# Logits of a soft mixture of experts: the token values as TensorE weights, the folded output columns moving

## The chip, the core and the metric

The kernel runs on one core of a Trainium2 chip. The core has a matrix engine (TensorE, PE in the rows; its weight loads are listed apart as PEld), a vector engine (VectorE, DVE), a scalar engine (ScalarE, ACT), a general one (GpSimd, POOL) and a queue that issues DMAs (SyncE, SP). A matmul on TensorE holds one operand still as weights and streams the other through it column by column; its result goes to PSUM, from which DVE and ACT read. The metric is the device time of one execution in microseconds, as the median of several.

## What is computed

Three stages: attention with query pooling, a gated unit (SiLU), and a soft mixture of experts whose dispatch and combine weights are two softmaxes of the same logits.

```python
def _moe_ref(x, w_gate, w_val, w_out):            # x: 2304 tokens x 512
    g = x @ w_gate                                # 512 x 1536
    silu = g * (1.0 / (1.0 + np.exp(-g)))
    return silu * (x @ w_val) @ w_out             # 1536 x 512

def _moe2_ref(x, phi, w1, w2):                    # phi: 512 x 32
    logits = x @ phi                              # 2304 x 32
    d = softmax(logits, over tokens)              # dispatch
    slot_input = d.T @ x                          # 32 slots x 512
    slot_out = relu(slot_input @ w1) @ w2         # 8 experts, 4 slots each
    c = softmax(logits, over slots)               # combine
    return c @ slot_out
```

## The kernel before

The 16 attention steps (4 batches, 4 pairs of heads) run first, each some 40 us long. From step 4 on the gated unit is woven into them, by a pace table that says how many of its pieces are due by which step; what is left runs alone after the last step. The experts come at the end ("the tail").

The gated unit goes through the 2304 tokens in 9 blocks of 256 tokens, and in a block through 6 slices of 256 hidden units (`block_slice`). A slice is 24 matmuls for g and 24 for v (lines 738, 742, 743: 128x256 values moving through 128x128 weights), then a tanh on ACT (749), three element-wise steps on DVE (750, 761, 779) and a cast on ACT (777). They leave the slice's values `h` as a high half `hh` in bfloat16 and a low half `hs[:, 1]` in float16, 128 hidden units on the partitions, two such groups `ci`, 256 tokens along the free axis. A slice's values go two ways:

- By a transposing DMA (780) into `Hn`, which holds a whole block. At the block's end `block_sums` multiplies it by the dispatch weights (matmuls `G`, line 905, added up into `G_acc` on DVE, 910). There is one buffer of `Hn` and there are two of `hs`.
- Into the logits, through `W2S`: w_out times phi, folded beforehand, as a high and a low half of 32 columns each, so 64 columns for a group of 128 hidden units. `slice_logits` (and `slice_last` for the last slice of all) issues four matmuls into a PSUM tile `lp` and DVE adds that to `La` (820, 822; 804 for the last).

In the logits matmuls of before the columns of `W2S` are the weights and the 256 tokens move: group 0 lands on PSUM partitions 0 to 63, group 1 on 64 to 127, and the 32 columns for the low halves on 0 to 31 and 64 to 95. So `La` is 128 partitions of 256 tokens, with four partial sums of each logit on four groups of 32 partitions. `SELW`, a stack of four scaled identities, adds the four up: at a block's end (`block_end`) a matmul with `SELW` as weights (846) gives `L`, 32 slots of 256 tokens, for the dispatch softmax; in `combine` a matmul for each 128 tokens with `La` as weights and `SELW` moving (920) gives `lt`, 128 tokens of 32 slots, for the combine softmax. Both are float32, which the trace shows as two instructions for each matmul.

The order of instructions on each engine isn't the order of the code: a scheduler places them by its own estimate of when each is ready, under the dependences that the code adds (`behind`, `not_before`). `stages` is a list of pieces of work that a slice leaves behind; one is issued at each step of the next slices, so that a slice's logits come while the next slice's g and v run.

Of the kernel before, what the change touches and what calls it, by code (L numbers as in the profile page):

```python
# [11 lines left out]
F32 = mybir.dt.float32  # L12
# [4 lines left out]
AF = mybir.ActivationFunctionType  # L17
ALU = mybir.AluOpType
AX = mybir.AxisListType
# [5 lines left out]
WSC = 256.0  # L25
HSC = 2.0**14
W2SC = 64.0
DSC = 1024.0
HB = 2
HI_DVE, LO_PART = 0.0, 1.0  # L30
# [33 lines left out]
MXB, STB, PVB, TRB, MMB = 2, 2, 1, 1, 2  # L64
# [13 lines left out]
def tile_pool_attention_glu_softmoe(  # L78
# [35 lines left out]
    def ps(tag, shape, dtype=F32, bufs=1, name=None):  # L114
        return psum.tile(shape, dtype, tag=tag, bufs=bufs, name=name or tag)
# [4 lines left out]
    id16 = const.tile([P, P], F16, name="id16")  # L120
    SEL = const.tile([P, NS], F32, name="SEL")
    CN = const.tile([P, 2, NS], F32, name="CN")
    SELW = const.tile([P, NS], F32, name="SELW")

    marks = []

# [9 lines left out]
    def selections():  # L136
        for z in range(P // NS):
            r = slice(z * NS, (z + 1) * NS)
            nc.gpsimd.tensor_copy(out=SEL[r, :], in_=id32[r, r])
        nc.gpsimd.tensor_scalar(SELW, SEL, 1.0 / (HSC * W2SC), None, ALU.mult)  # L140
        nc.gpsimd.memset(CN, 0.0)
        for z in range(2):
            r = slice(z * P // 2, (z + 1) * P // 2)
            nc.gpsimd.tensor_copy(out=CN[r, z, :], in_=SEL[r, :])
        nc.gpsimd.tensor_copy(out=id16, in_=id32)
# [3 lines left out]
    c_all = const.tile([P, NT // P, NS], F32, name="c_all")  # L149
    m_run = [const.tile([NS, 1], F32, name=f"m_run{i}") for i in range(2)]  # L150
    s_run = const.tile([NS, 1], F32, name="s_run")
    La = const.tile([P, BLK], F32, name="La")

    w_stack = ExitStack()
    wpool = ctx.enter_context(tc.tile_pool(name="wgv", bufs=1, side="left", reuse_waits="tile"))
# [611 lines left out]
    def behind(ins):  # L767

        if moe["done"] < late:
            after(ins, moe["mm"])  # L770

    def slice_halves(j, fp, Hn, h, hs, hh):
# [8 lines left out]
            out=Hn[:, fp].rearrange("p a c i f -> p (a c i) f"), in_=hs.rearrange("p a c n -> p (a c n)")  # L781
        ).ins.name

    def slice_last(j, fp, Hn, h, hs, hh):
        t = ps("tr", [P, BLK], bufs=TRB, name=f"lp{j}_{fp}")
        for ci in range(2):
            w = W2S[:, 2 * fp + ci]
            r = slice(ci * 2 * NS, (ci + 1) * 2 * NS)
            nc.scalar.copy(hh[:, ci, :], h[:, ci])
            if ci:  # L790
                warm(0, moe["mm_last"])
            nc.tensor.matmul(
                t[r, :], w.rearrange("p a s -> p (a s)"), hh[:, ci, :], start=True, stop=False, skip_group_check=True
            )
            nc.vector.tensor_tensor(out=hs[:, 1, ci], in0=h[:, ci], in1=hh[:, ci, :], op=ALU.subtract)
            mm = nc.tensor.matmul(
                t[ci * 2 * NS:ci * 2 * NS + NS, :], w[:, 0, :], hs[:, 1, ci, :], start=False, stop=True,
                skip_group_check=True,
            )
            moe["mm_last"] = mm  # L800
        moe["turn"] = nc.sync.dma_start_transpose(
            out=Hn[:, fp].rearrange("p a c i f -> p (a c i) f"), in_=hs.rearrange("p a c n -> p (a c n)")
        ).ins.name
        nc.vector.tensor_tensor(out=La, in0=La, in1=t, op=ALU.add)

    def slice_logits(j, fp, hs, hh):

        t = ps("tr", [P, BLK], bufs=TRB, name=f"lp{j}_{fp}")
        for ci in range(2):
            w = W2S[:, 2 * fp + ci].rearrange("p a s -> p (a s)")  # L810
            behind(nc.tensor.matmul(
                t[ci * 2 * NS:(ci + 1) * 2 * NS, :], w, hh[:, ci, :], start=True, stop=False, skip_group_check=True
            ))
        for ci in range(2):
            r = slice(ci * 2 * NS, ci * 2 * NS + NS)
            nc.tensor.matmul(
                t[r, :], W2S[:, 2 * fp + ci, 0, :], hs[:, 1, ci, :], start=False, stop=True, skip_group_check=True
            )
        if fp == 0:
            nc.vector.tensor_copy(out=La, in_=t)  # L820
        else:
            nc.vector.tensor_tensor(out=La, in0=La, in1=t, op=ALU.add)
# [16 lines left out]
    def block_end(j):  # L839
        mp = moe["pool"]  # L840
        Hn = moe[j]["Hn"]
        if j == NBLK - 1:
            warm(1, moe["mm_last"])
        tg, bf = ("mx", MXB) if j >= late else ("tr", TRB)
        L = ps(tg, [NS, BLK], bufs=bf, name=f"L{j}")
        mm = nc.tensor.matmul(L, SELW, La, start=True, stop=True)
        behind(mm)
        if j == NBLK - 1:
            warm(2, mm)

# [8 lines left out]
        nc.vector.tensor_scalar(ng, new, -1.0, None, ALU.mult)  # L859
        dT = h_tile(f"dT{j}")[1][:NS, :BLK]  # L860
        sb = mp.tile([NS, 1], F32, tag="sb", bufs=1, name=f"sb{j}")
        al = None
        if j:
            al = mp.tile([P, 1], F32, tag="al", bufs=2, name=f"al{j}")
            nc.scalar.activation(al[:NS, :], old, AF.Exp, bias=ng)
        nc.scalar.activation(dT, L, AF.Exp, bias=ng, accum_out=sb)
# [48 lines left out]

    def combine(j, mp):

        t = ps("tr", [P, 2, NS], bufs=TRB, name=f"lt{j}")
        for i in range(2):
            nc.tensor.matmul(t[:, i, :], La[:, i * P:(i + 1) * P], SELW, start=True, stop=True)  # L920
        cm = mp.tile([P, 2, 1], F32, tag="cm", bufs=1, name=f"cm{j}")
        nc.vector.tensor_reduce(out=cm, in_=t, axis=AX.X, op=ALU.max)
        ce = mp.tile([P, 2, NS], F32, tag="ce", bufs=1, name=f"ce{j}")
        nc.vector.tensor_tensor(out=ce, in0=t, in1=cm.to_broadcast([P, 2, NS]), op=ALU.subtract)
        nc.scalar.activation(ce, ce, AF.Exp)
# [380 lines left out]
```

## Time and profile before

| | before |
|---|---|
| median of 3 runs (lowest to highest) | 865.88 us (865.73 to 868.37) |
| span of the profiled execution | 863.9 us |
| PE busy, share of the span | 816.8 us, 95% |
| DVE, ACT, POOL busy | 541.2, 392.5, 414.0 us |

Times in the rows are microseconds from the span's start, in one profiled execution. Matmuls overlap: the busy time of one (0.27 us for 256 columns) is its latency, and what it takes of the engine is read from its start to the start of the next. A bracket at a row's end is the engine's idle time before it and what ended that.

### The profile page before, as it was taken

Reading aid. Unit: us, or ns where it says so; the run is one execution under the profiler, and the core shown is the slowest. Engines: PE = TensorE matmul, PEld = TensorE weight load, DVE = VectorE, ACT = ScalarE, POOL = GpSimd, SP = SyncE. Lnnn points to the kernel's source line nnn. Section 1 sums busy time; section 2 is a strip of 40 time slices with the busy share of each in tenths; the row PEclk is TensorE's granted clock in tenths of the full one; section 3 lists DMA queues with packets and bytes.
Section 4 is the critical chain, followed back from the end, with each engine's and each line's share of the span. In section 5 each row is a group of like instructions: output and inputs, shape, how many; then the busy total and the mean of one; then the engine's idle time right before and its main releaser. Section 6 shows DMA issues by size and latency. Waiting matters only on the chain.

```text
span 863.9 us, 23702 instructions
## 1 busy us (share of the span) xinstructions
PE 816.8 (95%) x9952; PEld 580.0 (67%) x9952; DVE 541.2 (63%) x1060; ACT 392.5 (45%) x739; POOL 414.0 (48%) x380
## 2 busy tenths in 40 slices
PE   5888898999999999999999999999999999998997
PEld 1455566777666767677776777676777777776345
DVE  6878779678888675666657575666723444445223
ACT  3455678677778444343434344344434211212112
POOL 7878667465768545564564556565445100000100
PEclk9999999999999999999999999999999999999998
DMA  6562678959759433424544445324012598457999
GB/s 194 149 153 84 200 214 239 284 127 280 192 173 293 115 61 82 111 76 100 130 115 120 111 107 125 65 26 97 16 28 38 149 292 267 85 165 193 297 290 292
DMA packets 151868, 132.48 MB, mean 153 GB/s; under 512 B 83152, under 2 KB 120720, under 8 KB 151760
## 3 DMA queue, kind: packets, MB, share of 16 engines
q1 hardware_dynamic: 149600, 130.92, 57.8%
q8 instruction: 78, 1.28, 0.6%
q10 hardware_dynamic: 2160, 0.04, 0.1%
q14 instruction: 30, 0.25, 0.1%
HBM read 84.10 MB, written 7.86 MB: 106 GB/s over the span
## 4 chain that ended last, share of the span: by engine, by line
PE 75%; DVE 12%; DMA 7%; ACT 3%; issue 2%; SPq 0%; ACTq 0%; DVEq 0%
PE st L462 7%; PE st L461 7%; PE mx L380 6%; PE g L738 5%; PE g L743 5%; PE g L742 5%; PE v L738 5%; PE v L743 5%; PE v L742 5%; DVE mp L386 3%; PE pv L497 3%; PE pv L505 3%; PE pv L506 3%; PE pv L507 3%; PE hp L1179 2%
## 5 line engine op out<-in xcount | busy, mean ns | idle before, releaser
L474 POOL TENSOR_TENSOR PL<-P 128x512 f16<-128x512 f32 (+1 forms) x311 | 326.0, 1061 | 230.0 <-ACT P L467 227.7
L467 ACT ACTIVATE P<-st 128x512 f32<-128x512 f32 (+1 forms) x336 | 191.4, 582 | 207.0 <-PE st L462 174.1
L386 DVE TENSOR_REDUCE mp<-mx 128x1 f32<-128x512 f32 x270 | 179.9, 684 | 55.9 <-PE mx L380 53.0
L461 PE MATMUL st<-QQ,KK 128*128 128x512 f16 (+1 forms) x576 | 143.7, 291 | 5.1 <-ACT P L467 4.3
L462 PE MATMUL st<-QH,KL 65*128 65x512 f16 (+1 forms) x576 | 144.4, 293 | 2.7 <-DMA QH<-mt 2.7
L505 PE MATMUL pv<-VV,P 128*128 128x65 f16 x1088 | 136.8, 193 | 4.9 <-DVE x L537 4.8
L506 PE MATMUL pv<-VV,P 128*128 128x64 f16 x1088 | 136.7, 195 | 0.0
L507 PE MATMUL pv<-VV,PL 128*128 128x65 f16 x1088 | 134.6, 192 | 0.0
L738 PE MATMUL g<-xT,wgv 128*128 128x256 f16 x432 | 118.6, 275 | 3.3 <-DVE hs L750 3.0
L505 PEld LDWEIGHTS <-P 128*128 128x128 bf16 x1088 | 103.9, 98 | 25.3 <-DVE x L537 6.5
L743 PE MATMUL g<-xT,wgv 128*128 128x256 f16 x432 | 118.5, 274 | 0.5 <-DVE wgv L703 0.5
L742 PE MATMUL g<-xT,wgv 128*128 128x256 f16 x432 | 118.6, 274 | 0.0
L738 PE MATMUL v<-xT,wgv 128*128 128x256 f16 x432 | 117.9, 273 | 0.0
L743 PE MATMUL v<-xT,wgv 128*128 128x256 f16 x432 | 117.8, 273 | 0.0
L742 PE MATMUL v<-xT,wgv 128*128 128x256 f16 x432 | 117.7, 273 | 0.0
L507 PEld LDWEIGHTS <-PL 128*128 128x128 f16 x1088 | 103.7, 99 | 13.5 <-issue 4.4
L506 PEld LDWEIGHTS <-P 128*128 128x128 bf16 x1088 | 103.2, 98 | 10.4 <-issue 2.2
L380 PE MATMUL mx<-kh,QD 128*128 128x512 f16 x270 | 103.8, 402 | 6.6 <-DVE mp L386 3.1
L738 PEld LDWEIGHTS <-wgv 128*128 128x128 f16 x864 | 85.1, 98 | 18.6 <-issue 2.1
L742 PEld LDWEIGHTS <-wgv 128*128 128x128 f16 x864 | 84.8, 98 | 18.4 <-issue 4.1
L743 PEld LDWEIGHTS <-wgv 128*128 128x128 f16 x864 | 84.8, 98 | 16.1 <-issue 0.8
L462 PEld LDWEIGHTS <-KL 65*128 65x128 f16 x576 | 51.7, 99 | 33.0 <-issue 14.9
(184 smaller groups left out, 1192.4 us busy)
## 6 DMA issues: line engine op xcount, KB each, us to landing
w<-in_w SPq DMA_DIRECT2D x16, 1024.0 KB, 7.6
w<-in_w SPq DMA_DIRECT2D x64, 256.0 KB, 5.5
vr<-in_vP SPq DMA_DIRECT2D x16, 585.0 KB, 5.1
KK<-kh SPq DMA_DIRECT2D x62, 144.0 KB, 2.6
qr<-in_qT SPq DMA_DIRECT2D x15, 576.0 KB, 3.9
kr<-in_kT SPq DMA_DIRECT2D x15, 576.0 KB, 4.2
r<-in_w_out SPq DMA_DIRECT2D x12, 512.0 KB, 4.3
r<-in_w_gate SPq DMA_DIRECT2D x24, 256.0 KB, 5.1
```

The source lines that it names most:

```text
L380: nc.tensor.matmul(t, q, kh[:, k0:k0 + kw], start=True, stop=True)
L386: nc.vector.reduce_max(out=mp[:, g, c:c + 1], in_=t, axis=AX.X)
L461: nc.tensor.matmul(t[:, o:o + w], KK[:, k], QQ[:, q0:q0 + w], start=True, stop=False)
L462: nc.tensor.matmul(t[:, o:o + w], KL[:, k], QH[:, q0:q0 + w], start=False, stop=True)
L467: marks.append(nc.scalar.activation(P32[:, :o], t[:, :o], AF.Exp, scale=1.0 / 16.0).ins.name)
L474: eng.tensor_tensor(out=PL[:, :o], in0=P32[:, :o], in1=PH[:, :o], op=ALU.subtract)
L505: nc.tensor.matmul(dst[:, :D + 1], PH[:, q], VV[:, c, 0, :], start=first, stop=False, skip_group_check=True)
L506: nc.tensor.matmul(dst[:, :D], PH[:, q], VV[:, c, 1, :D], start=False, stop=False, skip_group_check=True)
L507: nc.tensor.matmul(dst[:, :D + 1], PL[:, q], VV[:, c, 0, :], start=False, stop=(c == NCH - 1), skip_group_check=True)
L738: mm = nc.tensor.matmul(o, w[:, 0, d, f], xh, start=(d == 0), stop=False)
L742: nc.tensor.matmul(o, w[:, 0, d, f], xl, start=False, stop=False)
L743: nc.tensor.matmul(o, w[:, 1, d, f], xh, start=False, stop=(d == ND - 1))
```

## The change

The two operands of the logits matmuls change places. A new function `logits_of` takes 128 tokens of a group's half as weights and moves the folded columns through them: 64 for the high half, 32 for the low. A slice has eight matmuls instead of four. Both groups of hidden units add up in one PSUM tile, which is now `[128 tokens, 2 token groups, 2 halves of W2S, 32 slots]`: 128 values on a partition instead of 256. `La` has the same shape, in which a token's logit is the sum of two values on the same partition.

`block_end` adds these two on DVE into a new tile `Lt` (128 tokens by 2 groups by 32 slots), and two matmuls with `Lt` as weights and the identity moving give `L` as before. `combine` reads `Lt` as it is; its matmuls and its PSUM tile are gone. `SELW` is gone too, and its scale `LSC` goes into the activations.

```diff
+    La = const.tile([P, 2, 2, NS], F32, name="La")
+    Lt = const.tile([P, 2, NS], F32, name="Lt")
...
+    def logits_of(t, fp, ci, a, hx, first, last):
+        w = W2S[:, 2 * fp + ci]
+        for i in range(2):
+            tok = hx[:, i * P:(i + 1) * P]
+            if a:
+                mm = nc.tensor.matmul(t[:, i, 0, :], tok, w[:, 0, :], start=False, stop=last, skip_group_check=True)
+            else:
+                mm = nc.tensor.matmul(
+                    t[:, i].rearrange("p a s -> p (a s)"), tok, w.rearrange("p a s -> p (a s)"),
+                    start=(first and i == 0), stop=False, skip_group_check=True,
+                )
+            if i == 0:
+                behind(mm)
+        return mm
...
     def slice_logits(j, fp, hs, hh):
-        t = ps("tr", [P, BLK], bufs=TRB, name=f"lp{j}_{fp}")
+        t = ps("tr", [P, 2, 2, NS], bufs=TRB, name=f"lp{j}_{fp}")
         for ci in range(2):
-            w = W2S[:, 2 * fp + ci].rearrange("p a s -> p (a s)")
-            behind(nc.tensor.matmul(
-                t[ci * 2 * NS:(ci + 1) * 2 * NS, :], w, hh[:, ci, :], start=True, stop=False, skip_group_check=True
-            ))
+            logits_of(t, fp, ci, 0, hh[:, ci, :], ci == 0, False)
         for ci in range(2):
-            r = slice(ci * 2 * NS, ci * 2 * NS + NS)
-            nc.tensor.matmul(
-                t[r, :], W2S[:, 2 * fp + ci, 0, :], hs[:, 1, ci, :], start=False, stop=True, skip_group_check=True
-            )
+            logits_of(t, fp, ci, 1, hs[:, 1, ci], False, ci == 1)
...
     # block_end
-        mm = nc.tensor.matmul(L, SELW, La, start=True, stop=True)
-        behind(mm)
+        nc.vector.tensor_tensor(out=Lt, in0=La[:, :, 0, :], in1=La[:, :, 1, :], op=ALU.add)
+        for i in range(2):
+            mm = nc.tensor.matmul(
+                L[:, i * P:(i + 1) * P], Lt[:, i, :], id32, start=(i == 0), stop=(i == 1), skip_group_check=True
+            )
+            behind(mm)
...
     # combine
-        t = ps("tr", [P, 2, NS], bufs=TRB, name=f"lt{j}")
-        for i in range(2):
-            nc.tensor.matmul(t[:, i, :], La[:, i * P:(i + 1) * P], SELW, start=True, stop=True)
-        nc.vector.tensor_reduce(out=cm, in_=t, axis=AX.X, op=ALU.max)
+        nc.vector.tensor_reduce(out=cm, in_=Lt, axis=AX.X, op=ALU.max)
```

With this the scheduler also places other work differently. The places that matter here lie at the end of block 7 (blocks count from 0) and the start of block 8. The names carry block and slice: `lp8_1` is the logits tile of slice 1 of block 8, `G7_2` the last of the block sums of block 7, `g8_3` and `v8_3` the gate and value products of slice 3.

On PE before, the logits of slice 1 come right behind the last block sum of block 7 (a second pair from line 816 and the rest of `g8_3` follow):

```order
L905 LDWEIGHTS dS7_13406
L905 MATMUL G7_2_13441<-Hn7_12867,dS7_13406 32x256
L811 LDWEIGHTS W2S_70
L811 MATMUL lp8_1_13536<-hs8_1_13529,W2S_70 64x256
L811 LDWEIGHTS W2S_70
L811 MATMUL lp8_1_13536<-hs8_1_13529,W2S_70 64x256
L816 LDWEIGHTS W2S_70
L816 MATMUL lp8_1_13536<-hs8_1_13529,W2S_70 32x256
```

On PE now, they come one block sum earlier, behind `G7_1` (two more such pairs follow, one for each 128 tokens, and four pairs from line 790 with 32 columns moving):

```order
L911 LDWEIGHTS dS7_13592
L911 MATMUL G7_1_13613<-Hn7_13024,dS7_13592 32x256
L792 LDWEIGHTS hs8_1_13716
L792 MATMUL lp8_1_13723<-W2S_69,hs8_1_13716 128x64
L792 LDWEIGHTS hs8_1_13716
L792 MATMUL lp8_1_13723<-W2S_69,hs8_1_13716 128x64
```

The weights of a logits matmul are now the token values `hs8_1`, and what moves is 64 or 32 columns of `W2S`; the position moved from behind `G7_2` to behind `G7_1`. On PE now, behind `G7_2` the products of slice 3 follow at once:

```order
L911 LDWEIGHTS dS7_13592
L911 MATMUL G7_2_13627<-Hn7_13024,dS7_13592 32x256
L738 LDWEIGHTS wgv3_83
L738 MATMUL g8_3_13804<-xT8_931,wgv3_83 128x256
L742 LDWEIGHTS wgv3_83
L742 MATMUL g8_3_13804<-xT8_931,wgv3_83 128x256
```

Nothing of the logits stands between `G7_2` and `g8_3` any more.

On DVE before, at the end of block 7 the maximum `mb7` over `L` follows the last addition to `La`; the combine softmax (`cm7` and so on, from `lt7`) stands 15 rows further down, between block sums:

```order
L822 TENSOR_TENSOR La_76<-La_76,lp7_5_13357 128x256
L853 TENSOR_REDUCE mb7_13378<-L7_13376 32x1
L857 TENSOR_TENSOR m_run1_74<-m_run0_73,mb7_13378 32x1
L859 TENSOR_SCALAR ng7_13381<-m_run1_74 32x1
L868 COPY al7_13385<-al7_13385 32x1
```

On DVE now, the sum `Lt` and the whole combine softmax stand ahead of that maximum:

```order
L824 TENSOR_TENSOR La_75<-La_75,lp7_5_13537 128x128
L848 TENSOR_TENSOR Lt_76<-La_75 128x64
L925 TENSOR_REDUCE cm7_13641<-Lt_76 128x2
L927 TENSOR_TENSOR ce7_13643<-Lt_76,cm7_13641 128x64
L930 TENSOR_REDUCE cs7_13646<-ce7_13643 128x2
L931 TENSOR_SCALAR cs7_13646<-cs7_13646 128x2
L932 RECIPROCAL cs7_13646<-cs7_13646 128x2
L933 TENSOR_TENSOR c_all_71<-ce7_13643,cs7_13646 128x64
L859 TENSOR_REDUCE mb7_13564<-L7_13560 32x1
```

The combine softmax moved up by a stretch of block sums, to where DVE would wait for `L`.

## Rows read from the trace of the kernel before

**Rows 1.** The page: busy time of the engines, and TensorE's granted clock in tenths

```profile
PE 816.8 (95%) x9952; PEld 580.0 (67%) x9952; DVE 541.2 (63%) x1060; ACT 392.5 (45%) x739; POOL 414.0 (48%) x380
...
PEclk9999999999999999999999999999999999999998
```

**Rows 2.** Stretches: length, busy us (instructions) of PE, PEld, DVE, ACT, POOL; clock; DMA; GB/s

```profile
320.00:640.00 320.00, 318.88 (x3983) 234.15 (x3981) 201.86 (x387) 134.57 (x250) 174.32 (x152) 1.00 0.39 88
...
681.00:797.00 116.00, 112.55 (x1043) 88.13 (x1042) 54.90 (x125) 24.41 (x49) 0.00 (x0) 0.99 0.76 207
797.00:864.00 67.00, 57.96 (x714) 30.89 (x713) 18.44 (x73) 12.48 (x26) 2.52 (x15) 0.97 1.04 289
```

**Rows 3.** Waits of PE, 320 to 640 us: for whom, us, times, longest

```profile
PE mx L380 <- DVE mp L395: 0.8, 2, 0.4
PE dt L882 <- ACT dT L866: 0.2, 1, 0.2
```

**Rows 4.** Waits of PE, 640 to 797 us, the longest

```profile
PE g L738 <- DVE hs L750: 3.0, 3, 2.2
```

**Rows 5.** Stretches, instructions on `lp` alone: length, PE busy, DVE busy, clock, DMA

```profile
184.00:320.00 136.00, 3.05 (x22) 2.49 (x6) 1.00 0.73 192
320.00:640.00 320.00, 16.01 (x104) 10.89 (x26) 1.00 0.39 88
640.00:797.00 157.00, 12.35 (x88) 9.22 (x22) 0.99 0.61 161
```

**Rows 6.** PE in order of time at one slice's logits: start, duration, instruction

```profile
490.01 0.27 PE L743 MATMUL g<-xT,wgv 128*128 128x256 f16 x1
490.21 0.30 PE L811 MATMUL lp<-hs,W2S 128*64 128x256 bf16 x2
490.44 0.29 PE L816 MATMUL lp<-hs,W2S 128*32 128x256 f16 x2
490.66 0.43 PE L380 MATMUL mx<-kh,QD 128*128 128x512 f16 x1
```

**Rows 7.** PE in order of time: first and last of twelve attention matmuls

```profile
185.09 0.19 PE L505 MATMUL pv<-VV,P 128*128 128x65 f16 x1
...
185.43 0.19 PE L507 MATMUL pv<-VV,PL 128*128 128x65 f16 x1
```

**Rows 8.** PE in order of time at one block's `lt`

```profile
688.42 0.63 PE L920 MATMUL lt<-SELW,La 128*128 128x32 f32 x4
688.89 0.27 PE L742 MATMUL v<-xT,wgv 128*128 128x256 f16 x1
```

**Rows 9.** All engines in order of time, start of block 8

```profile
774.59 0.30 PE L811 MATMUL lp<-hs,W2S 128*64 128x256 bf16 x2
774.70 3.21 SPq L780 DMA_TRANSPOSE Hn<-hs  x2
...
775.03 0.28 PE L743 MATMUL g<-xT,wgv 128*128 128x256 f16 x1
...
779.12 0.60 ACT L749 ACTIVATE hs<-g 128x512 f32<-128x512 f32 x1 [9.45 <-DMA Hn<-hs]
...
780.49 0.27 PE L738 MATMUL g<-xT,wgv 128*128 128x256 f16 x1 [2.23 <-DVE hs L750]
```

**Rows 10.** Chain of work that ended last, from the last slice on: start, us, what

```profile
796.41 0.43 DVE La L804
796.88 0.63 PE L L846 x2
797.54 0.42 DVE mb L853
...
799.50 0.21 DVE dS L885
...
808.24 0.30 DVE siT L1132
...
829.90 0.37 PE lt L920 x4
```

More of the change, by code (lines that the diff above doesn't have):

```diff
@@ L27 @@
 W2SC = 64.0
+LSC = 1.0 / (HSC * W2SC)
 DSC = 1024.0
@@ L122, in tile_pool_attention_glu_softmoe @@
     CN = const.tile([P, 2, NS], F32, name="CN")
-    SELW = const.tile([P, NS], F32, name="SELW")
     marks = []
@@ L139, in selections @@
             nc.gpsimd.tensor_copy(out=SEL[r, :], in_=id32[r, r])
-        nc.gpsimd.tensor_scalar(SELW, SEL, 1.0 / (HSC * W2SC), None, ALU.mult)
         nc.gpsimd.memset(CN, 0.0)
@@ L151, in tile_pool_attention_glu_softmoe @@
     s_run = const.tile([NS, 1], F32, name="s_run")
-    La = const.tile([P, BLK], F32, name="La")
+    La = const.tile([P, 2, 2, NS], F32, name="La")
+    Lt = const.tile([P, 2, NS], F32, name="Lt")
     w_stack = ExitStack()
@@ L782, in slice_halves @@
         ).ins.name
+    def logits_of(t, fp, ci, a, hx, first, last):
[12 more added lines that the diff above has]
+        return mm
     def slice_last(j, fp, Hn, h, hs, hh):
-        t = ps("tr", [P, BLK], bufs=TRB, name=f"lp{j}_{fp}")
+        t = ps("tr", [P, 2, 2, NS], bufs=TRB, name=f"lp{j}_{fp}")
         for ci in range(2):
-            w = W2S[:, 2 * fp + ci]
-            r = slice(ci * 2 * NS, (ci + 1) * 2 * NS)
             nc.scalar.copy(hh[:, ci, :], h[:, ci])
@@ L791, in slice_last @@
                 warm(0, moe["mm_last"])
-            nc.tensor.matmul(
-                t[r, :], w.rearrange("p a s -> p (a s)"), hh[:, ci, :], start=True, stop=False, skip_group_check=True
-            )
+            logits_of(t, fp, ci, 0, hh[:, ci, :], ci == 0, False)
             nc.vector.tensor_tensor(out=hs[:, 1, ci], in0=h[:, ci], in1=hh[:, ci, :], op=ALU.subtract)
[L796 to L800, printed above, removed]
+            moe["mm_last"] = logits_of(t, fp, ci, 1, hs[:, 1, ci], False, ci == 1)
         moe["turn"] = nc.sync.dma_start_transpose(
@@ L806, in slice_logits @@
     def slice_logits(j, fp, hs, hh):
-        t = ps("tr", [P, BLK], bufs=TRB, name=f"lp{j}_{fp}")
+        t = ps("tr", [P, 2, 2, NS], bufs=TRB, name=f"lp{j}_{fp}")
         for ci in range(2):
-            w = W2S[:, 2 * fp + ci].rearrange("p a s -> p (a s)")
-            behind(nc.tensor.matmul(
-                t[ci * 2 * NS:(ci + 1) * 2 * NS, :], w, hh[:, ci, :], start=True, stop=False, skip_group_check=True
-            ))
+            logits_of(t, fp, ci, 0, hh[:, ci, :], ci == 0, False)
         for ci in range(2):
-            r = slice(ci * 2 * NS, ci * 2 * NS + NS)
-            nc.tensor.matmul(
-                t[r, :], W2S[:, 2 * fp + ci, 0, :], hs[:, 1, ci, :], start=False, stop=True, skip_group_check=True
-            )
+            logits_of(t, fp, ci, 1, hs[:, 1, ci], False, ci == 1)
         if fp == 0:
@@ L858, in block_end @@
         ng = mp.tile([NS, 1], F32, tag="ng", bufs=1, name=f"ng{j}")
-        nc.vector.tensor_scalar(ng, new, -1.0, None, ALU.mult)
+        nc.vector.tensor_scalar(ng, new, -LSC, None, ALU.mult)
         dT = h_tile(f"dT{j}")[1][:NS, :BLK]
@@ L864, in block_end @@
             al = mp.tile([P, 1], F32, tag="al", bufs=2, name=f"al{j}")
-            nc.scalar.activation(al[:NS, :], old, AF.Exp, bias=ng)
-        nc.scalar.activation(dT, L, AF.Exp, bias=ng, accum_out=sb)
+            nc.scalar.activation(al[:NS, :], old, AF.Exp, bias=ng, scale=LSC)
+        nc.scalar.activation(dT, L, AF.Exp, bias=ng, scale=LSC, accum_out=sb)
         if j:
@@ L916, in combine @@
     def combine(j, mp):
-        t = ps("tr", [P, 2, NS], bufs=TRB, name=f"lt{j}")
-        for i in range(2):
-            nc.tensor.matmul(t[:, i, :], La[:, i * P:(i + 1) * P], SELW, start=True, stop=True)
         cm = mp.tile([P, 2, 1], F32, tag="cm", bufs=1, name=f"cm{j}")
-        nc.vector.tensor_reduce(out=cm, in_=t, axis=AX.X, op=ALU.max)
+        nc.vector.tensor_reduce(out=cm, in_=Lt, axis=AX.X, op=ALU.max)
         ce = mp.tile([P, 2, NS], F32, tag="ce", bufs=1, name=f"ce{j}")
-        nc.vector.tensor_tensor(out=ce, in0=t, in1=cm.to_broadcast([P, 2, NS]), op=ALU.subtract)
-        nc.scalar.activation(ce, ce, AF.Exp)
+        nc.vector.tensor_tensor(out=ce, in0=Lt, in1=cm.to_broadcast([P, 2, NS]), op=ALU.subtract)
+        nc.scalar.activation(ce, ce, AF.Exp, scale=LSC)
         cs = mp.tile([P, 2, 1], F32, tag="cs", bufs=1, name=f"cs{j}")
```

## Prediction

> **What bounds the kernel now.** I read the page first, then the stretches in which logits are made, then PE's waits there, then single slices in order of time. The page says that PE is busy for 95% of the span at a full granted clock nearly throughout [rows 1]; as busy times of pipelined matmuls overlap, this alone proves little. The stretches say more: from 320 to 640 us PE is busy for 318.88 of 320 us, while DVE, ACT and POOL have 202, 135 and 174 us [rows 2]. In these 320 us PE waits for 1.0 us in all [rows 3]. So there the end is set by what PE has to issue, and a microsecond of PE work taken out should come back nearly whole. From 640 to 797 us, where the gated unit ends up running alone, the largest wait is 3.0 us for `g L738` [rows 4]; where its longest part comes from is told below. The tail after 797 us holds no logits but one `lt` [rows 2, 10].
>
> **What a slice's logits cost now.** The last matmul ahead starts at 490.01 [rows 6]. Products of 256 columns follow each other every 0.11 us where nothing else intervenes (the 27 from 775.03 to the wait run so [rows 9]), so the next one could start at 490.12. The two high-half matmuls start at 490.21, the two low-half ones at 490.44, and the next foreign one at 490.66. The four hold PE for 490.66 - 490.12 = 0.54 us. Two matmuls of one pair run side by side (0.30 us for both, hardly more than the 0.27 us of one product), but ahead of each pair PE stands about 0.1 us longer than its columns explain. Where a pair is torn apart by other work it costs more, and the stretches of these matmuls alone hold the mean [rows 5]: 3.05 + 16.01 + 12.35 = 31.4 us of PE for 22 + 104 + 88 = 214 matmuls, nearly all the 216 of 54 slices, or 0.58 us a slice. (These busy times leave out the 0.1 us ahead and take in some 0.07 us of overlap behind; for the slice above the busy time, 490.21 to 490.73, is 0.52 us against 0.54 [rows 6].)
>
> **What they will cost.** Eight matmuls a slice, each with 128 columns of 16-bit weights and 64 or 32 columns moving. The nearest rows are the attention's: the same weights, bfloat16 or float16 values of 128 columns, with 64 or 65 columns moving. Twelve of them start between 185.09 and 185.43 [rows 7]: 0.34 / 11 = 0.031 us each. I take 0.030, as half of the new ones move only 32 columns: 0.24 us a slice. At the low end the weight load could be all that counts, and no row shows a run below 0.031; at the high end stand the float32 matmuls `lt`, also with 128 columns of weights, at (688.89 - 688.42) / 4 = 0.117 us [rows 8]. I take the value of the 16-bit rows, since type, shape and engine state are the same. Sum: 54 x (0.58 - 0.24) = **18.4 us** off PE.
>
> One rule speaks against the change here. The rows show that the narrow weights of before did not give their pairs for nothing: 0.54 us where two streams of 256 columns would take 0.22. The Trainium skill, TensorEngine Tiling (Array Packing), section Performance Considerations, recommends just what before does for a moving side of at most 64 columns: swap it to be the weights and use column tiles. By that rule the slice would stand at 0.22 us now and at 0.24 after, and the sum would be +1 us instead of -18. The trace disagrees with it by the 0.32 us that it doesn't count.
>
> **The block's end.** `lt` is dropped: 0.47 us [rows 8], less where its first weight load is hidden (I take 0.42), in 8 blocks, 3.4 us; the ninth stands on the chain with 0.37 us [rows 10]. Together **-3.8 us**. `L` is now two matmuls of 128 columns instead of one of 256, in float32 twice as many instructions with the same columns in sum: 0.63 us on the chain [rows 10] becomes between 0.6 and 0.75; I take +0.05 in nine blocks, **+0.4 us**. `Lt` is a new DVE step of 128x64 float32; a step of that size takes 0.21 us (`dS`), and the addition to `La` shrinks from 0.43 to about 0.30, as `siT`, 128x128 from PSUM, does [rows 10]. `L` waits for it, and behind `L` on PE the next slice's g. In seven blocks the order puts some 3 us of products between the last logits and `L`, which hide it. In block 5, the last that follows attention work, and in block 8 nothing stands between but, in block 8, four dummy matmuls: there +0.21 + 0.06 - 0.13 = 0.14 us each, **+0.3 us**. That the combine softmax now stands ahead of the maximum on DVE adds seven small steps of some 0.2 us and a trip to ACT, about 1.4 us, to a stretch in which DVE would wait for `L`; its cover is the 3 us of products, and without it block ends would lose up to 1.4 us each. DVE's lighter additions (54 x 0.13 = 7 us) fall on an engine that isn't the bound: nothing. The dropped `SELW` step on POOL, done once at the start, and the scale in the activations: nothing.
>
> **The starts of blocks 7 and 8.** Here a fixed chain rules. The transposing DMAs of the new block's first slices may write `Hn` only after the last block sum; they start at 774.70, the tanh that needs a free `hs` runs at 779.12, and PE's next g at 780.49, after a wait of 2.2 us [rows 9]. Block 7's start shows the same with a shorter wait (it is among the three [rows 4]). From the last block sum to that g the time is the DMA's, whatever PE does. Before, `lp8_1` lay within it and cost nothing; now it lies ahead of the last block sum and costs 0.24 us, where the sum above books a gain of 0.34. **+1.2 us** for two blocks. PE's idle time there grows from 2.2 to about 2.8 us. I leave the clock out, as it is at 0.99 over the stretch already [rows 2].
>
> **Where it isn't whole.** The six slices before 320 us lie in a stretch with somewhat more waits, and a shortened PE meets the latencies of others sooner. I take 5% of the gain, **+1.0 us**. The tail's loads need memory that the gated unit frees; their queue moves forward with it, so the tail (67 us, DMA share 1.04, [rows 2]) shifts as a whole.
>
> Sum: -18.4 - 3.8 + 0.4 + 0.3 + 1.2 + 1.0 = -19.3 us. The profiled execution goes from 863.9 to about 844.6; the median of the runs lies 2.0 us above that span, and I carry the difference: 865.9 - 19.3 = 846.6, said as **846.5 us**.
>
> **Rivals.** *The weight loads bind (slower).* If a load of 128 token columns isn't hidden behind 64 moving ones, each of the 432 matmuls costs what `lt` costs, 0.117 us [rows 8]: 54 x (0.94 - 0.58) = +19.4, less 3.8 for `lt`, plus 1: 882 us. The change turns into a loss where a matmul takes more than (31.4 + 3.8) / 432 = 0.081 us. Against it: the twelve in 0.34 us [rows 7], whose weights are produced by ACT and POOL a little earlier as these are. For it: nothing in the trace but the float32 rows. The Trainium skill, TensorE: Matmul & The Clock Gate, section LDWEIGHTS (loading the stationary operand), would give this result: it has a load grow with its columns, an estimate of 107 ns for 128; its section on weight-path modes excepts 16-bit weights of just 128 columns, and by the twelve [rows 7] the exception holds. Chance 5%.
>
> *Others take over.* The gain is booked on PE, but the slices' chain over ACT, DVE and the transposing DMA is as long as before. If the wait at a block's start [rows 9] spreads to most block starts, or the new order costs attention waits, half is lost: 846.5 + 10 = about 856 us. For it: the 2.2 us wait is there already, and the order of about a quarter of DVE's instructions changes. Against: 1.0 us of waits in 320 us. Chance 20%.
>
> *PE's busy time is no bound at all (no change).* Then the end is set by something that the waits don't show, and the time stays at 865 to 867. Against it stands the 1.0 us of waits [rows 3]. Chance 4%.
>
> *More comes back.* The torn pairs, the 0.1 us ahead of each, and a kinder order give 24 to 27 us: 840 us. Chance 11%.
>
> **How the numbers follow.** My forecast, 842 to 851, has 60%. The range should leave out no more than 2 in 10: from 839, which takes in most of the better case, to 858, which takes in most of the absorbed one; it leaves out the loss and the unchanged time. A measurement of this kernel tells about 0.3% (2.6 us) from no change. Faster by more: 0.60 + 0.20 + 0.11 = 0.91; within: 0.04; slower: 0.05.
>
> **What would show it.** Right: the `lp` instructions take some 13 to 17 us of PE over all stretches, eight logits matmuls start about 0.03 us apart, PE's waits from 320 to 640 stay under 3 us, `lt` is gone, and g at the start of block 8 still waits, for 2.5 to 3 us. Wrong: starts 0.1 us apart (the weight loads), waits of PE for `L`, `dt` or `hs` at block ends (the combine softmax ahead of the maximum), or a last slice that doesn't come some 19 us earlier.

## The result, and the profile after

The changed kernel takes 855.29 us in the median of four runs (852.20 to 859.29), against 867.12 us (865.73 to 868.92) for the kernel before on the same chip: a ratio of 0.986, with an interval of 0.982 to 0.989. It is faster by about 12 us, where 19.3 were forecast; the time lies inside the range, nearer to its upper end, and outside the 842 to 851 us that were given 60%. The profiled execution, the fastest of the four, spans 850.3 us against 863.9. The page of the changed kernel begins (busy time, share of the span and instructions of each engine; then TensorE's granted clock in tenths, one digit for each fortieth of the span):

```profile
PE 793.7 (93%) x10150; PEld 582.7 (69%) x10150; DVE 534.6 (63%) x1069; ACT 391.7 (46%) x739; POOL 415.7 (49%) x379
...
PEclk9999999999999999999999999999999998999998
```

PE's busy time fell by 23 us from that in [rows 1], more than forecast, but the span fell by only 13.6: PE's share of it went down from 95 to 93%. So PE got rid of its work and then stood still for some of the time won. The stretches, with the columns of [rows 2], say where:

```profile
320.00:640.00 320.00, 318.61 (x4248) 244.68 (x4246) 202.67 (x397) 139.61 (x260) 181.12 (x159) 1.00 0.38 90
...
681.00:797.00 116.00, 100.58 (x1031) 80.18 (x1032) 51.07 (x131) 22.99 (x47) 2.52 (x15) 0.96 0.76 200
```

From 320 to 640 us PE is as full as before, with 4248 instructions where there were 3983: here what PE was spared came back as time. From 681 to 797 (the last 16 us of it are now the tail) it is busy for 100.6 of 116 us, where it was 112.6, and the granted clock is 0.96 instead of 0.99. PE's waits from 640 to 797 us (for whom; us, times, longest) answer [rows 4]:

```profile
PE g L738 <- DVE hs L750: 10.2, 4, 4.1
PE si4p L1123 <- DVE GT L1115: 1.4, 1, 1.4
PE L L850 <- DVE Lt L848: 1.1, 2, 0.7
```

Three waits of 3.0 us for `g` became four of 10.2 us (`si4p` belongs to the tail). The four, in PE's order of time (idle time ahead and what ended it in brackets; from four narrow stretches):

```profile
682.28 0.28 PE L738 MATMUL g<-xT,wgv 128*128 128x256 f16 x1 [0.56 <-DVE hs L750]
...
710.22 0.37 PE L738 MATMUL g<-xT,wgv 128*128 128x256 f16 x1 [4.07 <-DVE hs L750]
...
727.01 0.27 PE L738 MATMUL g<-xT,wgv 128*128 128x256 f16 x1 [1.67 <-DVE hs L750]
...
766.50 0.37 PE L738 MATMUL g<-xT,wgv 128*128 128x256 f16 x1 [3.94 <-DVE hs L750]
```

Counted by the products for `g`, they stand ahead of slice 4 of block 6, slice 2 of block 7, slice 4 of block 7 and slice 4 of block 8. PE runs two slices ahead of `tanh`, so the waits ahead of slice 4 go with a block's first transposing DMAs: these are the block starts of the prediction, and in the kernel before they were 0.54 us at block 7 and 2.23 at block 8. Ahead of a slice 2 the kernel before has no wait above 0.2 us. Behind both waits of 4 us PE's granted clock is low: 0.50 from 709.5 to 714 us and 0.52 from 766.5 to 770, that is the lower of the two levels (1.2 instead of 2.4 GHz), and products that took 0.11 us each go at 0.21.

**The path through the blocks.** The profiled executions can be laid side by side at three points: the first `tanh` (L749) of block 6, the last addition to `La`, and the end.

| point | before, us | after, us | after is ahead by |
|---|---|---|---|
| first `tanh` of block 6 | 682.8 | 664.2 | 18.6 |
| last addition to `La` | 796.4 | 781.1 | 15.3 |
| end of the span | 863.9 | 850.3 | 13.6 |

By the steps of the prediction, blocks 0 to 5 should have given 13.4 us (36 slices at 0.34, five `lt` at 0.42, less 0.9 for `L`, `Lt` and the share of the 5%), blocks 6 to 8 another 5.6, and the tail 0.2. They gave 18.6, -3.3 and -1.7. So the two halves missed in opposite directions, and the one that has to be explained first is the loss of some 9 us in blocks 6 to 8 of this execution. By blocks (columns of [rows 2]) it looks so, first the kernel before and then the changed one, each from the first `tanh` of a block to the next and at last to the last `La`:

```profile
683.00:725.00 42.00, 42.00 (x395) 33.35 (x393) 18.25 (x41) 8.15 (x17) 0.00 (x0) 1.00 1.08 308
725.00:762.00 37.00, 36.27 (x342) 28.43 (x341) 17.67 (x38) 7.25 (x15) 0.00 (x0) 1.00 0.50 119
762.00:797.00 35.00, 32.28 (x294) 24.55 (x292) 18.05 (x40) 8.05 (x17) 0.00 (x0) 0.95 0.65 183
```

```profile
664.00:709.00 45.00, 40.97 (x427) 34.73 (x425) 17.69 (x43) 8.44 (x17) 0.00 (x0) 0.99 1.10 289
709.00:747.00 38.00, 35.11 (x354) 28.98 (x354) 17.35 (x39) 7.51 (x15) 0.00 (x0) 0.92 0.45 114
747.00:782.00 35.00, 30.18 (x318) 24.68 (x316) 16.32 (x35) 7.78 (x15) 0.00 (x0) 0.95 0.75 185
```

Not one of the three became shorter by more than 0.2 us, and block 6 took 3 us longer. In block 6 the DMA engines were full already in the kernel before (the last but one number: 1.08), beside a PE that was exactly full too. Twelve loads of expert weights of 1 MB are issued there in both kernels, from 2 us ahead of the block to its end. PE needs less time for the block now; the share of the transfers stays as high (1.10).

### The profile page after: what moved, and what is told of

The parts are those of the page before. It is cut to its first block, busy times and chain, and to the rows that moved or that the text cites. A ratio compares the mean times of both kernels' runs of the same rounds, so it can differ in the third digit from the quotient of the medians.

```text
span 850.3 us, 24106 instructions
## 1 busy us (share of the span) xinstructions
PE 793.7 (93%) x10150; PEld 582.7 (69%) x10150; DVE 534.6 (63%) x1069; ACT 391.7 (46%) x739; POOL 415.7 (49%) x379
## 4 chain that ended last, share of the span: by engine, by line
PE 74%; DVE 12%; DMA 8%; ACT 3%; issue 2%; SPq 0%; ACTq 0%; DVEq 0%
PE st L461 7%; PE st L462 7%; PE mx L380 6%; PE g L738 5%; PE g L743 5%; PE g L742 5%; PE v L738 5%; PE v L742 5%; PE v L743 5%; DMA Hn<-hs 3%; PE pv L506 3%; PE pv L505 3%; PE pv L507 3%; PE pv L497 3%; DVE mp L386 2%
## 5 line engine op out<-in xcount | busy, mean ns | idle before, releaser
L738 PE MATMUL g<-xT,wgv 128*128 128x256 f16 x432 | 119.7, 277 | 10.9 <-DVE hs L750 10.2
```

What stands on the lines that cost most here:

```text
L738: mm = nc.tensor.matmul(o, w[:, 0, d, f], xh, start=(d == 0), stop=False)
```

## The experiments

Three theories were on trial for the loss. **Q**: the loads set for block 6 hold up the transposing DMAs of its slices, so that the slices' chain falls behind PE. **F**: the fixed chain at a block's start (last block sum, transposing DMA, `tanh`, `hs`, `g`) costs more than was booked. **O**: the order on DVE, with the combine softmax ahead of the maximum and of the additions to `G_acc`, delays the chain. Each edit below is to the changed kernel unless it says otherwise; ratios are to the kernel before on the same chip.

**The changed kernel again** (`after2`).

> The changed kernel again, beside the others of this chip. In its first profile PE was 18.6 us ahead of before at slice 0 of block 6 (664 us) and only 13.5 us ahead at the end, with PE waits of 11.9 us between 680 and 767 us and two stretches of half clock. All theories: the same here, ratio to before 0.982 to 0.990, waits of 8 to 14 us for the gate product g in that stretch.

It took 854.48 us (850.13 to 856.82), ratio 0.988 (0.983 to 0.993). Its profiled execution, span 848.3, has the first `tanh` of block 6 at 665.3 and the last `La` at 778.0, with waits for `g` of 0.4, 1.6, 1.7 and 3.8 us in the same four places. So blocks 6 to 8 gave 1.0 us here where 5.6 were forecast: the loss is 4.6 us, about half of that in the first execution, and block 7's clock stayed up. That there is a loss in blocks 6 to 8 does not differ; its size does. The times spread over 7 us, which is no mark of the change: thirteen executions of the kernel before on this chip spread over 8.

**The loads spread wider** (`after_ldp7`).

```
-LD0, LDP = 1, 4
+LD0, LDP = 1, 7
```

One load is issued in every seven of the unit's steps instead of every four, so that nine instead of twelve fall on block 6.

> One number of the changed kernel: the 12 early expert loads of 1 MB are issued one for each 7 pieces of gated-unit work instead of one for each 4. Theory Q (transposing DMAs stand in the queue behind expert loads, so that hs and Hn come free late): PE's waits for g between 680 and 767 us fall from 11.9 us to under 7, one stretch of half clock goes, time 4 to 7 us under the changed kernel's. Rival F (a fixed chain at block starts, last block sum to transposing DMA to tanh, whatever the loads do): waits stay at 10 or more, same time within 2 us. Rival O (the combine softmax ahead of the maximum on DVE delays the block's end): the same as F.

It took 846.30 us (844.50 to 847.05), ratio 0.977 (0.974 to 0.981): 8 us better than the change alone on the same chip (854.48). Issues from `hs` and of the loads in block 6 (engine and operation, count, KB each, median us from issue to landing), first of the changed kernel and then of this one:

```profile
w<-in_w SPq DMA_DIRECT2D x12, 1024.0 KB, 9.0
...
Hn<-hs SPq DMA_TRANSPOSE x6, 7.4
```

```profile
w<-in_w SPq DMA_DIRECT2D x9, 1024.0 KB, 7.8
...
Hn<-hs SPq DMA_TRANSPOSE x6, 3.4
```

The transposing DMAs of block 6 land 3.4 us after their issue instead of 7.4. (In the kernel before it was 7.0; there PE was late enough to cover them.) Block 6 now lasts 38 us instead of 45, with PE full:

```profile
667.00:705.00 38.00, 38.00 (x406) 33.01 (x405) 18.10 (x42) 8.32 (x17) 0.00 (x0) 1.00 0.91 237
```

The wait ahead of block 7's slice 2 is gone; 5.9 us in three waits for `g` are left, up to 3.5 us ahead of block 8's slice 4. Q is right for a good part of the loss.

**The same edit in the kernel before** (`before_ldp7`).

> The same one number in the kernel of before, whose PE waits for g in that stretch are 3.0 us. Theory Q: little to win, 0 to 3 us faster; so the difference between the two layouts grows to 16 us or more. F and O: no change, and the difference stays at 12 us.

It took 865.25 us, ratio 0.999 (0.997 to 1.002): no difference. There PE was as late as the transfers, and its waits for `g` stay at 2.8 us. The edit is no gain of its own; it pays only once PE is quicker.

**The twelve loads put off** (`after_late`). They are issued behind the last block; four other loads of 1 MB, between 737 and 757 us, stay.

```
-LD0, LDP = 1, 4
+LD0, LDP = -1000, 4
...
+    while n < NEE + NEX:
+        load(n, moe["mark"])
+        n += 1
```

> The changed kernel with the 12 early expert loads put off until the last block is through, so that blocks 6 to 8 run without them; the tail then waits for 12 MB more, and the total gets longer by 20 to 45 us. What counts is the stretch from the first tanh of block 6 to the last addition to La, 117 us in the changed kernel. Theory Q: 105 to 109 us, PE's waits for g under 4 us. Rival F: waits for g at the starts of blocks 6, 7 and 8 stay, 2 to 4 us each, 112 us or more. Rival O: 117 us as it was.

It took 874.87 us in one run, as the tail then waits for its weights; what counts is blocks 6 to 8: from the first `tanh` of block 6 to the last `La` it is 109.3 us instead of 116.9. The transposing DMAs of block 6 land in 3.0 us in the median. Block 6 lasts 38 us with PE full. PE's waits from 640 to 797 us:

```profile
PE dt L888 <- ACT dT L872: 5.3, 1, 5.3
PE g L738 <- DVE hs L750: 5.1, 2, 3.4
```

Two waits for `g` remain, ahead of slice 4 of block 7 (1.7 us) and of block 8 (3.4 us). At the first no load is on the way, so it can't be Q: F exists too. At block 8 one is, issued at 750.2 us; its transposing DMAs, from 753.0, land in 4.9 and 4.4 us. (The wait for `dt` is in the last block, behind the loads moved there.)

**Block sums in three banks, and the wider loads** (`after_gmx7`). In blocks 6 and 7 the three block sums of a block go through the one PSUM bank of the tag `pv`; the edit lets two of the three use the two banks of `mx`, where those of the earlier blocks go. A sum then need not wait until the one before has been added to `G_acc`.

```
-            tg, bf = ("pv", PVB) if j >= late else ("mx", MXB)
+            tg, bf = ("pv", PVB) if j >= late and not f else ("mx", MXB)
```

> The changed kernel with the loads at one for each 7 pieces and, in blocks 6 and 7, the block sums G in three PSUM banks instead of one, so that the three stand in a row on PE and Hn comes free some 6 us of PE work earlier. Two causes were found for PE's waits for g: Q (transposing DMAs behind expert loads) at the starts of blocks 6 and 7, and F (last block sum, transposing DMA, tanh) at slice 4 of blocks 7 and 8, 1.9 and 3.6 us, which stay when the loads are slow or late. If F is right these two go (under 0.5 us each) and the time is 3 to 6 us under that of the kernel with slow loads, 840 to 843 us. If not (the waits come from DVE's or ACT's own order), they stay, at 846 us.

It took 840.01 us (833.35 to 844.19), ratio 0.969 (0.963 to 0.975), the best of all. The start of block 8 in the changed kernel, of PE, SP and ACT, in order of time within each engine:

```profile
752.44 0.51 PE L911 MATMUL G<-Hn,dS 128*32 128x256 bf16 x12
755.71 0.51 PE L911 MATMUL G<-Hn,dS 128*32 128x256 bf16 x12
758.99 0.51 PE L911 MATMUL G<-Hn,dS 128*32 128x256 bf16 x12
...
759.54 4.26 SPq L780 DMA_TRANSPOSE Hn<-hs  x2
...
765.13 0.60 ACT L749 ACTIVATE hs<-g 128x512 f32<-128x512 f32 x1 [12.15 <-DMA Hn<-hs]
```

and in this one:

```profile
743.96 1.17 PE L911 MATMUL G<-Hn,dS 128*32 128x256 bf16 x36
...
745.17 4.09 SPq L780 DMA_TRANSPOSE Hn<-hs  x2
...
750.42 0.60 ACT L749 ACTIVATE hs<-g 128x512 f32<-128x512 f32 x1 [5.05 <-DMA Hn<-hs]
```

In the changed kernel the three sums stand 3.3 us apart, and the transposing DMAs start behind the third. Here all 36 matmuls run in 1.17 us, and the DMAs start 1.2 us after the first. No wait for `g` is left among PE's waits from 640 to 797 us, of which the most is

```profile
PE L L850 <- DVE Lt L848: 1.1, 2, 0.7
```

and the blocks take 38, 36 and 28 us:

```profile
666.00:704.00 38.00, 38.00 (x407) 32.97 (x405) 18.23 (x42) 8.42 (x17) 0.00 (x0) 1.00 0.94 250
704.00:740.00 36.00, 36.00 (x390) 31.60 (x388) 17.95 (x42) 7.72 (x17) 0.00 (x0) 1.00 0.73 182
740.00:768.00 28.00, 26.21 (x298) 22.24 (x296) 15.54 (x32) 7.27 (x13) 0.00 (x0) 1.00 1.04 267
```

The granted clock is 1.00 in all three, and the DMA share in block 8 is 1.04 without a wait of PE for `g`.

**The banks alone** (`after_gmx`).

> The changed kernel with the block sums of blocks 6 and 7 in three PSUM banks, and the loads as they were. F alone is taken away: the waits at slice 4 of blocks 7 and 8 (1.8 and 4.0 us) go, those at the starts of blocks 6 and 7 (0.7 and 1.7 to 4.2 us, with those before the logits) stay: 847 to 850 us. If one cause hides behind the other (the loads then delay the next transposing DMAs instead), the sum is worth less than its parts: 851 us or more.

It took 843.62 us (839.46 to 846.85), ratio 0.974 (0.968 to 0.979). One wait is left, 4.2 us for `g` ahead of block 7's slice 2, where block 6's transfers come late. By the ratios to the kernel before on the same chip, the loads alone gain 7 us on the change, the banks alone 11, both 15. That is less than the sum, but by no more than the intervals allow, so it is not shown that one cause hides behind the other.

**Both edits in the kernel before** (`before_gmx7`).

> The same two edits in the kernel of before, whose waits for g are 0.8 and 2.3 us. F: 2 to 3 us faster than before, 862 to 863 us. With both obstacles out of the way on both sides the difference between the two layouts is what PE was spared: 20 to 24 us by the theory that all of it comes back; 12 to 16 us if something else holds the changed kernel too.

It took 861.33 us, ratio 0.994 (0.992 to 0.997), with no wait for `g` left. With these two obstacles out of the way on both sides, the change is worth 861.3 - 840.0 = 21.3 us, by the intervals known to some 6 us. The prediction's terms for PE, without those for waits, were 18.4 + 3.8 - 0.4 - 0.3 = 21.5; that the two agree so closely is luck, as the profiled executions are 25.4 us apart (862.4 and 837.0), 20.8 of it ahead of block 6, and the tail takes 2.1 back. Blocks 6 to 8 are the better test. Between the first `tanh` of block 6 and the last `La` the two kernels take 108.4 and 101.6 us: 6.8 less, where 18 slices and three `lt`, less 0.3 for `L` and `Lt`, should give 7.1.

**The combine softmax held back** (`after_comb`).

```
+        red = nc.vector.tensor_reduce(out=cm, in_=Lt, axis=AX.X, op=ALU.max)
+        if j < NBLK - 1:
+            after(red, moe["sums"])
```

Its first step waits until a block's first addition to `G_acc`.

> The changed kernel with the combine softmax held back on DVE until the first addition to G_acc of its block, where it stood before. Rival O (it delays the maximum and with it the block's end): PE's waits for g between 660 and 770 us fall from 7 to 12 us to under 4. Theories Q and F: they stay at 7 to 12 us.

It took 851.97 us in one run, within the change's own spread, and the waits for `g` stay: 8.9 us in three, up to 3.9. O falls: at block 7's end the maximum starts 3.4 us behind the last addition to `La` in both kernels (742.47 to 745.88 us in the changed one, 740.45 to 743.85 here), as DVE waits for `L` either way.

**The transposing DMAs from another queue** (`after_actT`). Q leaves open whether the DMAs stand behind the loads in SP's queue or share the DMA engines with them. From block 5 on they are issued by ACT.

```
-        moe["turn"] = nc.sync.dma_start_transpose(
+        moe["turn"] = (nc.scalar if j >= late - 1 else nc.sync).dma_start_transpose(
```

> The changed kernel with the transposing DMAs of blocks 5 to 8 issued from ACT's queue instead of SP's, loads and order as they were. If the transposing DMAs are late because they stand behind loads in one queue: from issue to landing 3 to 4 us instead of 7 to 10 in block 6, and PE's waits at the starts of blocks 6 and 7 go: 846 to 849 us. If it is the bandwidth that loads take on the 16 engines: 6 to 9 us to landing still, the waits stay: 852 to 857 us, or more where ACT stands still while it issues.

It took 867.28 us, ratio 1.000 (0.997 to 1.003): the whole gain is lost. The transposing DMAs of block 6 land after 12.8, 17.6, 5.4, 3.6, 3.0 and 14.3 us, and block 6 lasts 57 us:

```profile
668.00:725.00 57.00, 42.47 (x422) 35.33 (x420) 18.04 (x42) 8.09 (x17) 0.00 (x0) 0.89 0.89 256
```

A queue of their own doesn't help: they are late without standing behind a load. Nor was it ACT, which the first two held for 8.5 us: the `tanh` at 688.47 us came with the landing of the first (675.55 + 12.83), 4 us after ACT was free. That leaves the shared engines. But the load on them was not the same: six loads went out by 670 us, where on SP it had been four by 665 and the fifth at 678, behind two transposing DMAs. Bunched loads and the other queue are not told apart by this run.

**The matmuls halved** (`after_split`). The price of a logits matmul is measured by itself: each one with 64 moving columns becomes two with 32, with the same weights each time, so a slice has twelve instead of eight.

```
-                mm = nc.tensor.matmul(
-                    t[:, i].rearrange("p a s -> p (a s)"), tok, w.rearrange("p a s -> p (a s)"),
...
+                for y in range(2):
+                    mm = nc.tensor.matmul(
+                        t[:, i, y, :], tok, w[:, y, :],
```

> The changed kernel with each matmul of 64 moving columns made into two of 32, with the same weights loaded twice: 12 logits matmuls a slice instead of 8. If weight loads of 128 16-bit columns are hidden and a matmul costs 0.025 to 0.03 us: +0.1 us a slice, so block 6 starts some 4 us later than in the changed kernel (664 to 665 us), at 668 to 670. If a further load costs 0.1 us: 14 us later.

PE in order of time at a slice (start, us, instruction; x4 is four in a row), first of the changed kernel and then of this one:

```profile
490.39 0.27 PE L743 MATMUL g<-xT,wgv 128*128 128x256 f16 x1
490.50 0.28 PE L792 MATMUL lp<-W2S,hs 128*128 128x64 f16 x4
490.62 0.44 PE L380 MATMUL mx_r<-kh,QD 128*128 128x128 f16 x4
...
491.26 0.25 PE L790 MATMUL lp<-W2S,hs 128*128 128x32 f16 x4
491.36 0.19 PE L505 MATMUL pv<-VV,P 128*128 128x65 f16 x1
```

```profile
502.45 0.27 PE L743 MATMUL g<-xT,wgv 128*128 128x256 f16 x1
502.56 0.26 PE L793 MATMUL lp<-W2S,hs 128*128 128x32 f16 x4
502.66 0.44 PE L380 MATMUL mx_r<-kh,QD 128*128 128x128 f16 x4
```

Four matmuls of 64 columns hold PE for 490.62 - 490.50 = 0.12 us, four of 32 columns for 0.10, whether they are the low half or a split high half; nothing stands idle ahead of them. So four more a slice should cost 0.10 us, and the five blocks from the first slice of block 1 to the first of block 6 took 364.6 us instead of 360.8. By PE's starts the logits took 2.6 of these 3.9 us, 0.09 a slice; blocks 2 and 5 are longer by 3.2 and 2.3 us and the other three shorter, so the rest is order and not price. The total missed: 862.86 us in one run. Block 6 starts 15.5 us later than in the changed kernel (679.7 against 664.2), where the matmuls explain some 4; part of it comes back later, as the waits for `g` are shorter (5.1 us). The other 11 are lost in block 0, most of them between 200 and 320 us, where the scheduler put other work together: PE's waits from 184 to 320 us, first of the changed kernel and then of this one,

```profile
PE st L461 <- ACT P L467: 1.3, 4, 0.5
PE g L743 <- DVE wgv L703: 1.1, 2, 0.8
```

```profile
PE st L461 <- ACT P L467: 5.2, 6, 2.5
PE v L738 <- DVE wgv L703: 1.8, 1, 1.8
PE g L738 <- DVE wgv L703: 1.2, 1, 1.2
PE w2p L680 <- ACT r L674: 1.2, 1, 1.2
```

and PE is busy there for 125.6 of 136 us instead of 131.7, at a granted clock of 0.97 instead of 1.00. The size of a matmul is settled by this run; its total says something about the order of the work, not about the matmuls.

## Why the prediction was right, and where its sum failed

**What bounds the kernel**: right up to 640 us, where PE is full in both kernels. For the last three blocks it was read from one mean: the DMA share of 0.76 over 681 to 797 us [rows 2] is 1.08, 0.50 and 0.65 by blocks. In block 6 the transfers were a second bound at the same height as PE.

**What a slice's logits cost**: right for the new form, and for the old one too little was booked. A burst of the new form takes 0.12 + 0.10 = 0.22 us against 0.24 booked. The 0.58 for the old form came from busy times. Counted from start to start on PE (with the time ahead of a matmul, without waits), the 30 slices of blocks 1 to 5 take 19.4 us before and 7.3 after, 0.65 and 0.24 each; over all 54 slices 19.7 us were spared where 18.4 were booked. What lifts the mean over the 0.54 of a whole slice is the eight of 30 that are torn apart. A logits matmul that stands alone in the kernel before:

```profile
416.89 0.27 PE L743 MATMUL g<-xT,wgv 128*128 128x256 f16 x1
417.10 0.30 PE L811 MATMUL lp<-hs,W2S 128*64 128x256 bf16 x1
417.32 0.39 PE L462 MATMUL st<-QH,KL 65*128 65x512 f16 x1
```

It holds PE for 417.32 - 416.89 - 0.11 = 0.32 us, more than the 0.27 of a pair, so a slice in four pieces costs 1.28 us; of the new form one that stands alone still costs 0.03. The attention's row [rows 7] was the fitting one and the float32 row [rows 8] was not: weights of 128 columns of 16 bits cost 0.025 to 0.029 us a matmul. The rule of the Trainium skill, TensorEngine Tiling (Array Packing), section Performance Considerations, would have kept the old form, and the trace disagrees: the old form is dearer by 0.32 us a slice, by 0.41 with the torn ones. The rival of the weight loads (the Trainium skill, TensorE: Matmul & The Clock Gate, section LDWEIGHTS) needed 0.117 us a matmul for its price and 0.081 for a loss, and fell by a factor of four.

**The block's end**: right within what can be seen. `L` takes 0.64 us with four instructions on the last chain, against 0.63 [rows 10]; it waits 1.1 us for `Lt` in two places, where it waited 0.7 for `La` before (0.3 more was booked), and `lt` is gone.

**The signs set for it** came in part. The one for the logits was badly chosen. PE's busy time on `lp` is 26.4 us over the stretches of [rows 5], not 13 to 17, while the cost is as forecast: a burst of four shows 0.28 us of busy time for 0.12 us of progress, since every burst adds the latency of its last matmul. Starts measure cost here; busy sums don't. PE's waits from 320 to 640 us are 1.4 us, under the 3 that were named. But block 8's wait is 3.94 us instead of 2.5 to 3, and the last slice comes 15.3 us earlier and not some 19, which the prediction had named as a sign of being wrong.

**The starts of blocks 7 and 8**: this term was too small, and with it the 5%. Together they put 2.2 us on lost gain. Blocks 6 to 8 lost 9 us against the sum in one execution and 4.6 in the other, and taking the two obstacles away gave back some 15 us in the changed kernel and about 5 in the one before. Two things were missing. The last block sum of block 7 in the kernel before, on PE:

```profile
774.14 0.51 PE L905 MATMUL G<-Hn,dS 128*32 128x256 bf16 x12
```

- The chain that the step named is there, but it was taken as a constant, with 0.6 us more to wait at each start. The 0.6 came: at block 8 PE's work between the last block sum and the wait fell from 4.12 to 3.57 us. But the chain grew too. The way from that block sum to `g` was 780.49 - 774.14 = 6.35 us; it became 766.50 - 758.99 = 7.51. The 1.2 us between them are in the transposing DMAs: from their start to the `tanh` it is 4.42 us before [rows 9] and 765.13 - 759.54 = 5.59 after. So the wait grew from 2.23 us to 3.94, and block 7's, ahead of its slice 4, from 0.54 to 1.67. Why these DMAs took longer was not tried. The step also took the chain to start as early as it can; `after_gmx7` shows that the sums ahead of it queued for one bank.
- Q was not seen at all. Ahead of block 7's slice 2, where the kernel before waits 0.2 us, PE now waits 4.07 us in one execution and 1.6 in the other, since block 6's transfers, a second bound at 1.08 before, became the first as soon as PE had less to do.

The step "I leave the clock out, as it is at 0.99" fell with them. That mean hid a place as well: behind block 8's wait of 2.23 us the clock of the kernel before was at the lower level for 3.4 us, as it is now. New is the stretch at block 7: the lower level lasts from 708.5 to 715.3 us, and PE works in it from 710.2, 5.1 us at half the speed, so it costs some 2.5 us. The waits for `g` grew by 7.2 us where 1.2 were booked; with the 2.5 us of clock that is 8.5 of the 8.9 us lost in this execution. That the wait brought the clock down is how the rows lie, not something that a run varied by itself; the last section has what speaks for it and against it.

**Blocks 0 to 5** gave 18.6 us where 13.4 were booked. From block 1 to block 6 the gain was 15.0 us in the profiles of both runs of the change, against some 12. By the starts the logits gave 12.1 of it, where 30 x 0.34 = 10.2 were booked, and `lt` 1.9, so the term that was too small is the price of the old form; about 1 us is open. Ahead of block 1's first `tanh` nothing can be said: it comes between 303.4 and 306.9 us in the profiles of the changed kernel and its variants, leaving out `after_split`, and between 307.0 and 310.9 in the three with the old form, so a single pair of executions is not enough there. `after_split` shows that the scheduler's order alone can move ten times as much in that part of the kernel; no run here held the order still.

**The tail** lost another 1.7 us instead of shifting as a whole. The wait of `si4p` for `GT` grew by 1.1 us (0.3 before, 1.4 after), but it is 0.3 again in `after_ldp7` and `after_gmx7`, whose tails are longer than before all the same (68.9 and 69.5 us from the last `La` to the end, against 67.4). The cause is open.

**The rivals**: "others take over" was the one that came out in part. It named the wait at a block's start spreading to other starts and gave about 856 us; the kernel takes 855.3. That the number fits is luck, as it stood for half of the gain without a sum, while the profiled execution fell short of the sum by 9 us in blocks 6 to 8 and by 1.9 in the tail, and went 5 beyond it ahead of them. It is luck too that the forecast's own misses partly cancel. The forecast's mechanism stood on PE, this rival's stood on the chain, and both happened.

**More comes back**, the rival of the torn pairs, was right about the pairs: they are 1.9 of the 3 us that blocks 1 to 5 gave beyond the sum.

## What to carry to other kernels

When the bound engine is relieved, don't read the other resources as a mean over a long stretch: go block by block, and look for one that is already full beside it (a DMA share over 1), and for chains whose wait is short only because the bound engine is late. What such a place will take back can be measured by removing the obstacle in both kernels: here it was 5 us before the change and 15 after, and the two edits that gained 0.6% before the change gained 1.8% on top of it. In this kernel a matmul with 32 or 64 moving columns and 128 columns of 16-bit weights took 0.025 to 0.03 us from start to start, so here the token values could serve as weights without a penalty. Where the cost of an instruction is asked for, count from start to start, torn groups included.

## What was unexpected of the hardware

- A transposing DMA of block 6 landed in 3.0 us without the twelve loads, in 7.4 us beside twelve 1 MB loads in 45 us (289 GB/s), and in up to 17.6 us from a queue of its own against the same loads bunched. A second queue gave it no precedence. In the kernel before, those of block 5 landed in 2.7 us, in the changed one in 3.0 to 3.3; what the 0.3 us are is open.
- Pairs of matmuls with 64 and 32 columns of weights stood about 0.1 us ahead of each pair [rows 6], and a single one held PE for 0.32 us where a pair held it for 0.27; bursts with 128 columns of weights follow the product before them with no gap (490.39, 490.50).
- Eleven waits of PE for `g` between 3.33 and 6.73 us, over all profiled executions, were each followed by a stretch at the lower clock level. Of shorter ones, 2.23 us in the kernel before was, 2.18 in `before_ldp7` and 2.86 in `after_split` were not. And ahead of block 6's first product PE waits four times, 1.6 us in all, in the changed kernel and in `after_ldp7` alike: in the second the clock was 0.51 from 663.5 to 667 us, in the first it stayed at the upper level.
